# Regrouping the attention visits of a fused attention and maxout kernel, with one store per output tile

## The chip, the cores and the metric

The kernel runs on one core of a Trainium2 chip. The metric is the device time of one execution in microseconds (us). Profiles come from one execution each; their span is some 2 us shorter than the device time of the same execution. "State" below means whether an execution ran undisturbed (fast) or not (slow); with one core a profile shows that only through the time of the repeats, which agreed within about 1% unless said otherwise.

## The reference, cut to what matters

Eight batches, 12 heads, 448 positions, head width 64. A softmax attention with one extra term in the denominator is followed by a feed-forward layer that takes the maximum of three products ("experts").

```python
q, k, v: (8, 12, 448, 64) float32          # w1, w2, w3: (768, 768), w_out: (768, 768)

scores = (q @ k.T) / sqrt(64)
m = max(scores);  e = exp(scores - m)
attn = e / (sum(e) + exp(-m) + 1e-09)
x = (attn @ v) -> (3584, 768)              # batch and position by head and width
h = maximum(maximum(x @ w1, x @ w2), x @ w3)
out = h @ w_out                            # (3584, 768) float32
```

Of the kernel before, what the change touches and what calls it, by code (L numbers as in the profile page):

```python
# [16 lines left out]
MMDT = FP16  # L17
LAMBDA = 256.0


@with_exitstack
def kernel(
# [36 lines left out]
    LAST = 6  # L59
# [10 lines left out]
    ps_s = ctx.enter_context(tc.tile_pool(name="ps_s", bufs=3, space=bass.MemoryType.PSUM))  # L70
    ps_b = ctx.enter_context(tc.tile_pool(name="ps_b", bufs=2, space=bass.MemoryType.PSUM))

    ctx.enter_context(tc.manual_schedule())

# [97 lines left out]
    def warm(n, cols=512):  # L172
        ps = ps_b.tile([128, 512], FP32, tag="b", name="warm")
        for _ in range(n):
            nc.tensor.matmul(
                out=ps[:, 0:cols], lhsT=wz[:, 0:128], rhs=wz[:, 0:cols], start=True, stop=True
            )
# [14 lines left out]
    def transpose_pe(i, pr, pool, k_eng, q_engs):  # L192


        def tile_of():
            if pool is ps_s:
                return ps_s.tile([128, 2, 1024], MMDT, tag="s", name="trT")[:, 0]
            return ps_b.tile([128, 1024], MMDT, tag="b", name="trT")
# [23 lines left out]
    def transpose_once(i, nm, eng):  # L222

        if i not in KT:
            KT[i] = att_pool.tile([P, T * 128], MMDT, tag="KT", name="KT")
            QT[i] = att_pool.tile([P, (NB + 1) * 128], MMDT, tag="QT", name="QT")
        tp = ps_b.tile([128, 1024], MMDT, tag="b", name="trT")
        for b in range(T):
            nc.tensor.transpose(  # L229
                out=tp[:, ts(b, 128)],  # L230
                in_=raw[i][nm][:, 2 * b + 1 : 2 * b + 3, :].rearrange("x t d -> x (t d)"),
                identity=ident16,
            )
        dst = KT[i][:, 0 : T * 128] if nm == "k" else QT[i][:, 4 * 128 : (4 + T) * 128]
        evac(eng, dst, tp[:, 0 : T * 128])
# [54 lines left out]
    def scores(i, ej, units, part="EO"):  # L290
# [5 lines left out]
        for n in range(0, len(units), per):  # L296
            us = units[n : n + per]
            stp = ps_s.tile([128, 2, 512], FP32, tag="s", name="stp")
# [35 lines left out]
    def av_tail(i, ej, pr, ws=(0, 1, 2, 3)):  # L334

        eF, vt = e_buf[ej], vt_buf[i % NV]
        ps = ps_s.tile([128, 2, 512], FP32, tag="s", name="avp")
# [15 lines left out]
    def av_last(i, ej, pr):  # L353



        eF, vx, vt = e_buf[ej], v_buf[i % NV], vt_buf[i % NV]
        ps = avs[i, pr]

        def tile_mm(r, hh, o, rhs, stop):  # L360
            nc.tensor.matmul(  # L361
                out=ps[hh * HP : hh * HP + HP, r, 3 * D1 : 4 * D1],
                lhsT=eF[r * HP : r * HP + HP, o : o + HP],
                rhs=rhs,
                start=False,
                stop=stop,
                skip_group_check=True,
            )

        n = where[pr, None, TL]  # L370
        for hh in range(2):
            tile_mm(hh, hh, e_col(n, 3), vt[hh * HP : hh * HP + HP, pr, 0:D1], False)
        for c, x in enumerate((X1, X3, X2)):
            for r in range(2):
                for hh in range(2):
                    o = e_col(where[pr, hh, x], 3)
                    rhs = vx[r * HP : r * HP + HP, 2 * pr + hh, x[0], 0:D1]
                    tile_mm(r, hh, o, rhs, c == 2)

    def av_main(i, ej, pr, ws=(0, 1, 2, 3), last=False):  # L380
# [29 lines left out]
        if not last:  # L410
            return None
        end = small.tile([P, D1], FP32, tag="end", name="end")
        rl = small.tile([P, 1], FP32, tag="rl", name="rl")
        nc.scalar.activation(out=end, in_=ps[:, 1, 3 * D1 : 4 * D1], func=AF.Copy)  # L414

        def finish():
            nc.vector.tensor_tensor(out=end, in0=ps[:, 0, 3 * D1 : 4 * D1], in1=end, op=ALU.add)
            nc.vector.tensor_scalar(
                out=rl, in0=end[:, D:], scalar1=1.0 / LAMBDA, scalar2=None, op0=ALU.add
            )  # L420
            nc.vector.reciprocal(out=rl, in_=rl)  # L421
            for hh in range(2):
                h = slice(hh * HP, hh * HP + HP)
                nc.scalar.activation(  # L424
                    out=xn[i][0:HP, pr, 3, hh], in_=end[h, 0:D], func=AF.Copy, scale=rl[h]
                )

        return finish
# [14 lines left out]
    def x_transpose_pe(i, part):  # L443
# [3 lines left out]
        tp = ps_b.tile([128, NP, 2, 128], MMDT, tag="b", name="xtp")  # L447
# [10 lines left out]
    def x_transpose_all(i):  # L458
        b, g = groups[i]
        tp = ps_b.tile([128, NP, 4, 128], MMDT, tag="b", name="xtp")  # L460
# [20 lines left out]
    def up_piece(b, fcs, i, q0, qn):  # L481
# [5 lines left out]
        p_i = ps_b.tile([128, 512], FP32, tag="b", name="p_i")  # L487
# [18 lines left out]
    def out_piece(bp, t, c, w, queues):  # L506
# [5 lines left out]
        op_ps = ps_b.tile([128, 512], FP32, tag="b", name="op_ps")  # L512
# [12 lines left out]
        if queues is None:  # L525
            return
        for half in range(2):
            n = 2 * t + half
            b = 2 * bp + n // T
            rows = out[b * S : (b + 1) * S].rearrange("(p t) m -> t p m", t=T)[order[n % T]]  # L530
            queues[half].dma_start(
                out=rows[:, outs[1] : c + w], in_=o_sb[half * HP : half * HP + HP, outs[1] : c + w]
            )
        outs[1] = c + w
# [11 lines left out]
    def add_out(b):  # L546
        sy, sc = nc.sync, nc.scalar
        for t in range(0, 3) if b % 2 == 0 else range(3, 7):
            cuts = [(0, NW, None), (NW, NW, (sy, sy))]
            if b == B - 1 and t == 6:  # L550
                cuts = [(0, NW, (sy, sy)), (NW, 256, (sc, sc)), (NW + 256, 128, (sy, sc))]
            for c, w, queues in cuts:
                pieces.append((out_piece, (b // 2, t, c, w, queues), NFC * (w + 6)))
# [7 lines left out]
    def fill(cols):  # L561
        credit[0] += cols
        while pieces and credit[0] > 0:
            f, a, w = pieces.pop(0)
            f(*a)
            credit[0] -= w
        if not pieces:
            credit[0] = min(credit[0], 0.0)

    def one():  # L570
        if pieces:
            fill(max(0.0, 1.0 - credit[0]))
# [9 lines left out]
    def av(i, ej, pr, part):  # L582
        if i >= LAST:
            av_tail(i, ej, pr, (0, 1, 2))
            av_last(i, ej, pr)
            return av_main(i, ej, pr, (0, 1, 2), True)
# [24 lines left out]
    transpose_pe(0, 0, ps_s, DV, (AC, DV))  # L611
    attend("O", 0, S01)
    transpose_pe(0, 1, ps_b, DV, (DV,))
    attend("O", 0, S23, S46)
    warm(4)
    transpose_pe(1, 0, ps_b, AC, (DV,))
    transpose_pe(1, 1, ps_s, AC, (DV,))
# [5 lines left out]
    transpose_pe(2, 0, ps_b, AC, (DV,))  # L623
    transpose_pe(2, 1, ps_s, AC, (DV,))
# [34 lines left out]
    visits = ((0, 1), (2, 3), (4, 5, 6))  # L659
    adds = {3 * (3 * b + 4) + (b >= PE_X): b for b in range(1, B - 1)}  # L660
# [3 lines left out]
    def share(n):  # L664


        nxt = min([a for a in adds if a > n], default=3 * NI + 2)
        rest = range(n, nxt)
        sums = [AVC if m % 3 < 2 and m < 3 * NI else 0 for m in rest]
# [8 lines left out]
    for i in range(3, NI):  # L678
        ej, pj = (i + 1) % NEB, i % NEB
        first = i == 3  # L680
        if PE_QK <= i + 2 < NI:
            transpose_dma(i + 2)
        if first:
            load_v(i + 2)
        for vi, units in enumerate(visits):
            n = 3 * i + vi
            scores(i, ej, units)
            if i == 4 and vi == 0:
                prep_v(i, DV)
            finish = None  # L690
            if vi < 2:
                finish = av(i - 1, pj, vi, "E" if first else "EO")
            if n in adds:
                add_batch(adds[n])
            per = STEP if first and vi < 2 else share(n)
            if finish:
                one()
                finish()
            if vi == 1 and i > 3 * PE_X:
                x_transpose_dma(i - 1)  # L700
            if vi == 0 and first:
                x_transpose_pe(1, "E")
            if vi == 2 and first:
                x_transpose_pe(i - 1, "E")
                fill(per / 2)
                prep_v(i, DV)
                for w, cols in ((0, (0, NE)), (1, (0, NE)), (2, (NE, NO)), (2, (0, NE))):
                    add_up(0, *cols, [(w, f) for f in (0, 2, 4)])
                add_out(0)
                per = share(n)  # L710
            if vi == 2 and 3 < i <= 3 * PE_X:
                x_transpose_all(i - 1)
            if first:
                fill(per)
                per = 0
            if i + 1 < PE_QK and vi < 2:
                transpose_once(i + 1, "qk"[vi], (AC, DV)[vi])
            fill(per)
        if i + 1 < PE_QK:
            shift_q(i + 1, nc.gpsimd)  # L720
        if first:
            load_qk(i + 3)
        if i < 5:
            load_more(i + 3, i + 4)
        if 5 <= i + 1 < NI:
            prep_v(i + 1, nc.gpsimd)
        if PE_QK <= i + 2 < NI:
            shift_q(i + 2, nc.gpsimd)
        if i >= 5:
            load_more(i + 3, i + 4)  # L730

    for pr in range(NP):
        finish = av(NI - 1, NI % NEB, pr, "EO")
        one()
        finish()
    x_transpose_dma(NI - 1)
# [33 lines left out]
```

## The kernel before: the parts that the change and the argument touch

Everything is in 16-bit floats on TensorE, with float32 sums in PSUM. The heads are handled in groups of four (24 groups). The program is a hand-made schedule: **visits** of attention work (scores, exponentials, value products) alternate with **pieces** of feed-forward work from a list. There are two kinds of pieces: an expert piece is 6 matmuls of 448 columns, an output piece 6 matmuls of 384 columns. A third of a group's scores is worked on per visit, and the value products of a pair of heads in two of the three visits.

Two PSUM pools separate the two kinds of work; the sums of a visit never share a bank with a piece:

```python
ps_s = tc.tile_pool(name="ps_s", bufs=3, space=PSUM)     # scores and value sums, two banks each
ps_b = tc.tile_pool(name="ps_b", bufs=2, space=PSUM)     # pieces, one bank each
```

The value products of a pair. The last 64 queries (448 is 7 x 64, so one block of 64 is left over) come out as two half sums in two banks; ScalarE copies one, VectorE adds the other:

```python
def av_tail(...):   # small products: 64x64 tiles of TensorE
def av_last(...):   # the last 64 queries, in 64x64 tiles, two half sums
def av_main(i, ej, pr, ws, last=False):
    ...             # 18 wide products, 128x128
    # VectorE: rb = 1/(sum + 1/LAMBDA), then xn = acc * rb
    nc.scalar.activation(out=end, in_=ps[:, 1, 3 * D1 : 4 * D1], func=AF.Copy)
    def finish():
        nc.vector.tensor_tensor(out=end, in0=ps[:, 0, 3 * D1 : 4 * D1], in1=end, op=ALU.add)
        ...         # VectorE: rl = 1/(...); ScalarE: two scalings of 64x64
```

The output. One tile of `hT` holds 128 columns, that is two blocks of 64 positions; the positions of one block lie 7 rows apart in `out`. So each tile `o_sb` of 128 x 768 is stored as two transfers of 64 rows:

```python
def out_piece(bp, t, c, w, queues):
    ...             # 6 matmuls into a bank, VectorE scales into o_sb[:, c : c + w]
    for half in range(2):
        n = 2 * t + half
        b = 2 * bp + n // T
        rows = out[b * S : (b + 1) * S].rearrange("(p t) m -> t p m", t=T)[order[n % T]]
        queues[half].dma_start(out=rows[:, outs[1] : c + w],
                               in_=o_sb[half * HP : half * HP + HP, outs[1] : c + w])
```

SyncE (SP) issues these stores, and also the **DMA transposes**: transfers that turn a block of queries and keys (`QT<-ld_q`, `KT<-ld_k`) or of attention output (`xT<-xn`) on the way, so that TensorE need not do it.

The softmax here doesn't subtract the row's maximum and nothing guards it: scores larger than these inputs give would overflow.

## Time and profile before

| | before |
|---|---|
| device time, median of the first 3 runs (lowest to highest) | 339.3 us (338.11 to 339.39) |
| span of the profiled run | 336.9 us |
| mean granted TensorE clock | 0.999 |
| last matmul starts, end of the span | 331.38, 336.88 us |

The busy shares, the slices and the chain of waits of this kernel are in the prediction below. What the argument needs beside them are the clock row of the 40 slices (tenths of full speed in each), two rows of the list of DMA issues (KB of each, us from issue to landing), and TensorE's wait for a DMA transpose (us in total, how often, the longest):

```profile
PEclk9999999999999999999999999999999999999999
...
out_dram<-o_sb SPq DMA_DIRECT2D x54, 192.0 KB, 4.0
...
xT<-xn SPq DMA_TRANSPOSE x18, 4.8
```

```profile
PE p_i L490 <- DMA xT<-xn: 0.3, 1, 0.3
```

TensorE waits for a DMA transpose once, for 0.3 us.

```profile
L473 SPq DMA_TRANSPOSE xT<-xn x18: 1232/1233/2319, 85.3 to 300.1; - x18
```

### The profile page before, as it was taken

How to read it: one execution, taken by the hardware profiler on the slowest of the kernel's cores; microseconds unless marked ns; L12 is line 12 of the kernel's file. 1: busy time of each engine (PE TensorE's matmuls, PEld its weight loads, DVE VectorE, ACT ScalarE, POOL GpSimd, SP SyncE). 2: the span in 40 equal slices, each digit the busy share in tenths (PEclk: the TensorE clock that was granted, in tenths of full speed). 3: DMA queues.
4: the chain of work that ended last, by engine and by line, in shares of the span. 5: the costliest groups of instructions: out<-in, count | busy, mean ns of one | idle time of the engine just before them, and what ended most of it. 6: DMA issues, size and time to landing. Idle time of an engine off the chain costs nothing.

```text
span 336.9 us, 10248 instructions
## 1 busy us (share of the span) xinstructions
PE 326.1 (97%) x4316; PEld 195.9 (58%) x4316; DVE 199.9 (59%) x521; ACT 183.1 (54%) x289; POOL 146.7 (44%) x260
## 2 busy tenths in 40 slices
PE   7899999999999999999999999999999999999993
PEld 3668788866556655565546646555556555565552
DVE  4556675566566556556656556556556556575552
ACT  4768856655665755676556655666565665420000
POOL 8596578880671539170854328351754000000000
PEclk9999999999999999999999999999999999999999
DMA  8999999799799999969996999989990730124016
GB/s 141 197 200 207 203 205 191 128 161 191 109 108 132 171 234 145 124 96 190 177 156 81 114 259 120 150 99 220 186 149 18 164 89 2 31 47 129 0 33 157
DMA packets 84815, 46.46 MB, mean 138 GB/s; under 512 B 53280, under 2 KB 81312, under 8 KB 84768
## 3 DMA queue, kind: packets, MB, share of 16 engines
q0 software_dynamic: 29120, 21.80, 48.6%
q1 hardware_dynamic: 55264, 23.60, 41.3%
q8 instruction: 34, 0.56, 0.7%
q10 hardware_dynamic: 384, 0.39, 0.4%
q14 instruction: 13, 0.11, 0.1%
HBM read 44.04 MB, written 11.01 MB: 163 GB/s over the span
## 4 chain that ended last, share of the span: by engine, by line
PE 87%; DMA 5%; ACT 2%; DVE 2%; issue 1%; POOL 1%; POOLq 0%; ACTq 0%
PE p_i L490 48%; PE op_ps L514 14%; PE stp L304 11%; PE avp L388 9%; DMA xT<-xn 3%; ACT e L324 2%; DMA ld_q<-in_q_dram 2%; PE avp L344 2%; PE avp L361 1%; DVE xn L404 1%; PE trT L229 1%; DVE QT L190 1%; PE xtp L463 0%; ACT QT L188 0%; DVE rb L401 0%
## 5 line engine op out<-in xcount | busy, mean ns | idle before, releaser
L324 ACT ACTIVATE e<-stp 128x896 f16<-128x896 f32 (+4 forms) x171 | 143.9, 901 | 60.3 <-PE stp L304 60.1
L490 PE MATMUL p_i<-xT,w 128*128 128x448 f16 (+2 forms) x972 | 173.1, 332 | 0.5 <-DMA xT<-xn 0.3
L490 PEld LDWEIGHTS <-w 128*128 128x128 f16 x972 | 90.2, 98 | 69.1 <-issue 6.0
L249 POOL COPY QT<-QT 64x384 f16<-64x384 f16 (+1 forms) x84 | 46.9, 558 | 93.9 <-DMA QT<-ld_q 69.2
L501 DVE TENSOR_TENSOR hT<-hT,p_i 128x448 f16<-128x448 f16 (+2 forms) x96 | 59.7, 622 | 35.7 <-PE p_i L490 35.6
L514 PE MATMUL op_ps<-w,hT 128*128 128x384 f16 (+2 forms) x342 | 58.5, 323 | 0.0
L304 PE MATMUL stp<-QT,KT 64*64 64x448 f16 (+2 forms) x756 | 48.1, 338 | 2.6 <-ACT e L324 0.9
L499 DVE CAST hT<-p_i 128x448 f16<-128x448 f32 (+2 forms) x48 | 30.0, 625 | 25.2 <-PE p_i L490 25.2
L514 PEld LDWEIGHTS <-hT 128*128 128x128 f16 x342 | 32.0, 98 | 22.4 <-issue 2.0
L424 ACT ACTIVATE xn<-end,rl 64x64 f16<-64x64 f32 x72 | 24.9, 346 | 34.5 <-DVE rl L421 34.1
L521 DVE TENSOR_SCALAR o_sb<-op_ps 128x384 f32<-128x384 f32 (+2 forms) x57 | 31.2, 547 | 17.4 <-PE op_ps L514 16.8
L388 PE MATMUL avp<-vx,e 128*128 128x65 f16 x936 | 38.6, 194 | 0.0
L388 PEld LDWEIGHTS <-e 128*128 128x128 f16 x936 | 32.1, 97 | 2.3
L304 PEld LDWEIGHTS <-KT 64*64 64x64 f16 x756 | 15.8, 105 | 26.8 <-issue 23.9
L398 DVE TENSOR_SCALAR rb<-avp 128x6 f32<-128x6 f32 (+2 forms) x54 | 8.8, 164 | 36.8 <-PE avp L388 36.8
L404 DVE TENSOR_TENSOR xn<-avp,rb 128x384 f16<-128x384 f32 (+2 forms) x54 | 29.3, 543 | 1.8
L433 POOL COPY vx<-ld_v 128x768 f16<-128x768 f16 x21 | 17.2, 820 | 6.8 <-issue 4.2
L344 PEld LDWEIGHTS <-e 64*64 64x64 f16 x624 | 13.7, 107 | 8.1 <-issue 1.7
L102 POOL DMA_DIRECT2D ld_q<-in_q_dram x24 | 17.4, 723 | 2.3 <-DMA w<-in_moe_w_dram 1.1
L102 POOL DMA_DIRECT2D ld_k<-in_k_dram x24 | 17.3, 722 | 2.1 <-DMA w<-in_moe_w_out_dram 1.1
L414 ACT ACTIVATE end<-avp 128x65 f32<-128x65 f32 x36 | 8.2, 227 | 17.1 <-PE p_i L490 12.4
L115 POOL DMA_DIRECT2D ld_v<-in_v_dram x24 | 15.2, 634 | 2.6 <-DMA w<-in_moe_w_dram 1.3
(52 smaller groups left out, 162.1 us busy)
## 6 DMA issues: line engine op xcount, KB each, us to landing
out_dram<-o_sb SPq DMA_DIRECT2D x54, 192.0 KB, 4.0
ld_v<-in_v_dram POOLq DMA_DIRECT2D x48, 128.0 KB, 5.1
ld_k<-in_k_dram POOLq DMA_DIRECT2D x23, 224.0 KB, 6.6
ld_q<-in_q_dram POOLq DMA_DIRECT2D x23, 224.0 KB, 7.5
w<-in_moe_w_dram POOLq DMA_DIRECT2D x9, 384.0 KB, 9.2
w<-in_moe_w_out_dram POOLq DMA_DIRECT2D x3, 384.0 KB, 8.5
xT<-xn SPq DMA_TRANSPOSE x18, 4.8
QT<-ld_q SPq DMA_TRANSPOSE x17, 7.3
```

The source lines that it names most:

```text
L102: nc.gpsimd.dma_start(out=tiles[nm][:, 1 : NP * T + 1].rearrange("x (r t) d -> x r (t d)", r=NP)[:, p0:p1], in_=src[:, p0:p1],)
L249: eng.tensor_copy(out=t[d0 : d0 + HP, o * 128 : (o + n) * 128], in_=t[s0 : s0 + HP, a * 128 : (a + n) * 128],)
L304: nc.tensor.matmul(out=stp[half * HP : half * HP + HP, par, j * qn : (j + 1) * qn], lhsT=k_block(i, pr, h2, x[half]), rhs=q_cols(i, pr, h2 ...
L324: nc.scalar.activation(out=dst, in_=src, func=AF.Exp, scale=scale)
L388: nc.tensor.matmul(out=ps[:, hh, j * D1 : (j + 1) * D1], lhsT=eF[:, o : o + 128], rhs=vx[:, 2 * pr + hh, (x[0]), 0:D1], start=False, stop= ...
L404: nc.vector.tensor_tensor(out=xn[i][:, pr, ws[0] : ws[0] + nw].rearrange("p j h d -> p h j d"), in0=acc[:, :, :, 0:D], in1=rb.unsqueeze(3) ...
L424: nc.scalar.activation(out=xn[i][0:HP, pr, 3, hh], in_=end[h, 0:D], func=AF.Copy, scale=rl[h])
L490: nc.tensor.matmul(out=p_i[:, j * qn : (j + 1) * qn], lhsT=w_sb[i][:, dc, ts(fc, 128)], rhs=xT[b][:, dc, q0 : q0 + qn], start=(dc == 0), s ...
L499: nc.vector.tensor_copy(out=dst, in_=src)
L501: nc.vector.tensor_tensor(out=dst, in0=dst, in1=src, op=ALU.max)
L514: nc.tensor.matmul(out=op_ps[:, 0:w], lhsT=hT[bp][:, fc, ts(t, 128)], rhs=wout_sb[:, fc, c : c + w], start=(fc == 0), stop=(fc == NFC - 1),)
L521: nc.vector.tensor_scalar(out=o_sb[:, c : c + w], in0=op_ps[:, 0:w], scalar1=1.0 / LAMBDA, scalar2=None, op0=ALU.mult,)
```

## The change

Its intent has four parts: fewer, fuller visits from group 6 on (three groups, 21 score units, in seven visits of three units, where there were nine); all sums of a pair of heads in one PSUM bank, one of the two that pieces use, in turn; the last 64 queries of a pair scaled by VectorE straight from that bank, one piece later; and each output tile stored by one transfer. The core of the diff:

```diff
-    ps_s = ctx.enter_context(tc.tile_pool(name="ps_s", bufs=3, space=bass.MemoryType.PSUM))
-    ps_b = ctx.enter_context(tc.tile_pool(name="ps_b", bufs=2, space=bass.MemoryType.PSUM))
+    slots = [ps.tile([128, 2, 512], FP32, name=f"ps{j}") for j in range(3)]
+    banks = [ps.tile([128, 512], FP32, name=f"pb{j}") for j in range(2)]
...
+    def visit(units, pair):
...
+            for at in anti:                       # scores of the first unit on two of the four tiles
+                s0(*at)
+            turned = turn_over(smalls(diag, True))   # first half of the small products on the others
+            for s, at in ((s0, diag), (s1, anti), (s1, diag), (s2, anti), (s2, diag)):
+                for corner in at:
+                    s(*corner)
+            smalls(anti, False, turned)           # second half, behind a semaphore
...
+            wides()
...
         def finish():
+            for hh in range(2):
+                nc.vector.tensor_scalar(out=dst[0:HP, pr, 3, hh], in0=acc[h, 6, 0:D],
+                    scalar1=rb[h, 6:7], scalar2=None, op0=ALU.mult)
+            if pr == 1:
+                x_transpose_dma(pi)
+        if units:
+            return finish                         # called after the next piece
+        finish()
...
-        for half in range(2):
-            n = 2 * t + half
-            b = 2 * bp + n // T
-            rows = out[b * S : (b + 1) * S].rearrange("(p t) m -> t p m", t=T)[order[n % T]]
-            queues[half].dma_start(
-                out=rows[:, outs[1] : c + w], in_=o_sb[half * HP : half * HP + HP, outs[1] : c + w]
-            )
+        r0, r1 = ((2 * bp + n // T) * S + order[n % T] for n in (2 * t, 2 * t + 1))
+        cols = slice(outs[1], c + w)
+        for p0, r, k in ((0, r0, 2),) if r1 > r0 else ((0, r0, 1), (HP, r1, 1)):
+            at = out[r : r + 1, cols]
+            rows = bass.AP(
+                at.tensor, at.offset, [[abs(r1 - r0) * DM, k], [T * DM, HP], [1, c + w - outs[1]]]
+            )
+            queue.dma_start(out=rows, in_=o_sb[p0 : p0 + k * HP, cols])
```

The pattern in `out` has three dimensions, slowest first: `k` = 2 blocks, 64 rows, the columns. The bytes are those of the two transfers before. In one tile of seven the second block lies ahead of the first (`r1 < r0`), and that tile keeps two transfers.

## The prediction

That matmuls overlap is meant as the trace of before shows it: one of an expert product takes 352 ns there and the next starts 0.189 us after it. And a transpose on TensorE, put at 0.066 us in step 4, starts 0.056 us after the one ahead of it at the median of that trace.

> **What bounds the kernel now.** I read the page from the top: busy shares, the 40 slices, then the chain of work that ended last.
>
> ```profile
> PE 326.1 (97%) x4316; PEld 195.9 (58%) x4316; DVE 199.9 (59%) x521; ACT 183.1 (54%) x289; POOL 146.7 (44%) x260
> PE   7899999999999999999999999999999999999993
> DMA  8999999799799999969996999989990730124016
> PE 87%; DMA 5%; ACT 2%; DVE 2%; issue 1%; POOL 1%; POOLq 0%; ACTq 0%
> ```
>
> TensorE is 97% busy, full in all but the first two slices and the last, and carries 87% of the chain. Busy alone is weak evidence, since matmuls overlap, so I compared starts of consecutive matmuls in the trace: after the first 13 us no two lie more than 0.6 us apart, save once, at 194.3 us, where an expert product waited for a transpose (0.65 us instead of 0.19; the list of waits books 0.3 us). So the end is set by how densely TensorE's stream is packed. DVE, ACT and POOL have 40% and more to spare; a saving there is worth something only if TensorE waits for it. The DMA engines are full to about 280 us, but only that one wait shows.
>
> How dense is one visit? The timeline of TensorE over one of them (start, us, engine, line, operation), with the vector engine's part behind it:
>
> ```profile
> 201.61 0.35 PE L490 MATMUL p_i<-xT,w 128*128 128x448 f16 x1
> 201.90 0.57 PE L304 MATMUL stp<-QT,KT 64*64 64x448 f16 x8
> 202.30 0.26 PE L344 MATMUL avp<-vt,e 64*64 64x65 f16 x12
> 202.42 0.27 PE L361 MATMUL avp<-vx,e 64*64 64x65 f16 x10
> 202.62 0.74 PE L388 MATMUL avp<-vx,e 128*128 128x65 f16 x18
> 203.20 3.57 PE L490 MATMUL p_i<-xT,w 128*128 128x448 f16 x18
> ...
> 203.40 0.16 DVE L398 TENSOR_SCALAR rb<-avp 128x6 f32<-128x6 f32 x1 [0.78 <-PE avp L388]
> 203.60 0.19 DVE L401 RECIPROCAL rb<-rb 128x6 f32<-128x6 f32 x1
> 203.82 0.56 DVE L404 TENSOR_TENSOR xn<-avp,rb 128x384 f16<-128x384 f32 x1
> 204.53 0.62 DVE L499 CAST hT<-p_i 128x448 f16<-128x448 f32 x1 [0.15 <-PE p_i L490]
> ```
>
> A visit is a stretch in 64x64 tiles (scores, small value products), then 128x128 work: 18 wide value products, then expert pieces of 6 matmuls. Expert matmuls start every 0.189 us (18 in 3.40 us in the chain). The first score starts 0.29 us after the last expert matmul (201.61 to 201.90): **0.09 us to enter tile mode**. Starts in the trace give 0.124 us from the last small product to the first wide one where the cadence is 0.03: **0.09 us to leave it**; from a score straight to an expert piece it is 0.27 instead of 0.19, so 0.08. A set of four scores takes 0.19 us, 26 small products 0.23.
>
> [...]in this visit a small product starts at 202.395 on one tile, ahead of the one that precedes it in the program[...].[...]
>
> **The change, part by part.** I listed TensorE's instructions in both programs: 4316 matmuls each.
>
> 1. *Fewer visits.* Stretches in tile mode fall from 82 to 70: some 13 score-only ones go (an exit of 0.08 and an entry of 0.09 each), and the last pair of heads now needs two stretches instead of one. 12 x 0.18 = **2.2 us less**.
>
> 2. *Packing inside a stretch.* Each now holds three score units and both halves of the small products. The small ones on the diagonal tiles run beside the first unit's anti-diagonal scores. A diagonal tile has three scores (3 x 0.187) and 7 small products (7 x 0.031), 0.78 us; before, three units and a pair's small ones took 3 x 0.19 + 0.23 = 0.80. Over 37 such visits some **0.3 us less**, counting the entry effects.
>
> 3. *Semaphore between the two halves.* The second half (other row tiles, same bank) waits for a scalar-engine instruction that waits for the first half. From the stretch's start: first half done at 0.19 + 0.19 latency, then three steps of about 0.05 each (early scores start 0.05 after what releases them): 0.53 us. The second half is due at about 0.57. An estimate of **0.5 us more** for all visits.
>
> 4. *Group 5* takes the new form: 12 wide products fewer (0.03 each) and 8 PE transposes fewer (0.066 each): **0.9 us less**. Its transpose becomes a DMA, needed about 8 us after issue; landings of that kind take 4.4 to 8.6 us at that time.
>
> 5. *Scaling of the last 64 queries.* ACT loses 36 copies (8.2 us) and 72 scalings (24.9 us); DVE loses 36 x (218 + 154 + 164) ns = 19.3 us and gains 76 scalings of 64x64. Off TensorE's path, so nothing by itself. But the sums' bank is now one of the two that pieces use, and is free only after these scalings, which stand behind the first piece's copy. That is a **new wait**, and the program has it: the last piece of a visit waits for the second scaling. With U the first piece's start: its copy starts at U+1.33 (203.20 to 204.53) and takes 0.62. A scaling costs 0.225 us, an estimate from the PSUM forms of one op (292 ns at 128 columns, 425 at 256: 1.04 ns a column). So the bank is free at U+2.40, and TensorE restarts at U+2.45.
>  - In a visit of three 448-column pieces the third is due at U+2.27: 0.18 us lost. Program order shows 17 such: **3.1 us more**.
>  - Visits of four pieces or more lose nothing (due at U+3.09 or later).
>  - The first three new visits have only 1, 2 and 2 output pieces of 0.97 us. There the scalings end at about U+2.2 (the copy waits for the 0.56 us product that ends at U+1.18), while the next user of the bank is due at U+0.97 or 1.07: 1.2 + 1.3 + 1.3 = **3.7 us more**.
>
> 6. *The wait at 194 us* should go: a batch's pieces now begin 9.5 to 11 us after its last transpose is issued, 7.5 to 9.5 before. **0.4 us less**.
>
> 7. *Stores.* Six output tiles of seven go out in one transfer instead of two (the seventh's rows run backwards and keep two); bytes are equal. Hidden, except at the end:
>
> ```profile
> 330.10 3.88 SPq L531 DMA_DIRECT2D out_dram<-o_sb  x5
> 330.49 1.43 DVE L521 TENSOR_SCALAR o_sb<-op_ps 128x384 f32<-128x384 f32 x3 [0.42 <-DMA out_dram<-o_sb]
> ...
> 331.60 1.84 ACTq L531 DMA_DIRECT2D out_dram<-o_sb  x3
> ```
>
>  The last data are ready at 331.92, but the queue is still issuing and starts the last store at 333.51; it lands 2.1 us later. The tile ahead of the last still needs two transfers, the last one fewer: the last store should start some 0.6 to 1.0 us earlier. **0.6 us less**.
>
> Sum: -2.2 - 0.3 + 0.5 - 0.9 + 3.1 + 3.7 - 0.4 - 0.6 = +2.9 us, 342.2.
>
> **Rivals.**
> - *The waits are hidden, only the switches count.* For it: TensorE waits for almost nothing now, and the change was evidently laid out to keep it so. Against it: the waits are in the program, and their times follow from durations in the trace. It would give 339.3 - 4.4 + 0.5, about 335.5.
> - *Tile packing fails*: small products do not run beside longer scores on other tiles, or the semaphore takes longer. Up to 0.19 us in 37 visits, 7 us: about 346 to 349. The out-of-order start above speaks against it; no trace of before has unequal lengths side by side in different tiles for long.
> - *A transfer becomes the bound.* The DMA engines are 90% busy for most of the run. Shifted copies of the queries stay 12 us and more ahead of their use in the late groups (from the trace), so I give this little; group 5's transpose might cost 1 us.
> - *ACT or DVE relief brings time.* ACT is 54% busy and no TensorE wait of note ends on it: nothing.
>
> **Range and chances.** The mechanism sum is 342.2. The first rival pulls down by 6 us and I give it a quarter; packing failure pulls up by as much with about a tenth. I predict 341.0 us, with 336.5 to 345.0 for 8 in 10. Faster by over 2% needs 332.5, less than switches alone explain: 0.03. Slower by over 2% needs 346.1, the packing failure: 0.07. Within 2%: 0.90.
>
> **What would show it.** In the changed profile: 70 tile stretches with entry and exit still near 0.09; the scores' first part and the small products starting within 0.01 us of each other, and about 0.87 us from first score to first wide product; gaps of about 0.2 us before the third piece in 17 visits, listed as waits of the expert product on the vector engine, and three gaps of over 1 us near 80 to 90 us; scalings of about 0.22 us; no wait near 195 us; the last store issued within 1 us of the last copy. I am wrong if the expert products show no wait on the vector engine (then 335 to 337), or if the stretch takes over 1 us (then 346 and more).

## More of the kernel before

How long SP was held by each store and each transpose is in the two views by source line (minimum, median and maximum in ns, then the first and last start in us):

```profile
L531 SPq DMA_DIRECT2D out_dram<-o_sb x57: 466/587/1661, 70.0 to 333.5; - x57
```

## The result, and the profile after

| | before | after |
|---|---|---|
| device time, median (lowest to highest) | 339.16 us (338.11 to 339.39, 4 runs) | 428.28 us (426.27 to 431.2, 4 runs) |
| ratio after to before | | 1.264 (95% interval 1.256 to 1.272) |
| span of the profiled run | 336.9 us | 426.0 us |
| mean granted clock | 0.999 | 0.915 |
| last matmul starts, end of the span | 331.38, 336.88 us | 402.83, 426.01 us |

A ratio here is the mean time of one kernel's fast runs over that of the other's of the same rounds, so it is not quite the ratio of the medians that are quoted. Executions over 1.5% slower than the fastest of the same kernel are left out of the means. The change made the kernel 26% slower; the prediction had 0.5% and gave "slower by over 2%" a chance of 0.07.

The page of the changed kernel, the rows that answer to those shown before (busy shares, slices of TensorE, clock and DMA, the list of DMA issues):

```profile
PE 345.0 (81%) x4316; PEld 206.3 (48%) x4316; DVE 202.5 (48%) x488; ACT 149.8 (35%) x181; POOL 146.4 (34%) x260
...
PE   8899998609999989799496995949799997499800
...
PEclk9999999957999999999796996969989998879965
DMA  9999999999995959859898499993997292710121
...
out_dram<-o_sb SPq DMA_DIRECT2D x23, 384.0 KB
```

The same 4316 matmuls, but the row of TensorE now has holes, and behind most holes the clock row has a dip: 5, 7, 6. Two slices at the end are empty. TensorE's list of waits says what it stood for:

```profile
PE pb L595 <- DMA xT<-xn: 29.9, 5, 11.6
PE pb L482 <- issue: 6.2, 2, 4.0
PE ps L415 <- POOL QT L268: 5.4, 1, 5.4
PE ps L415 <- DMA KT<-ld_k: 5.0, 1, 5.0
PE pb L619 <- DVE xn L524: 2.3, 2, 1.1
```

Transposes that land late head it: of attention output (`xT`), of queries (`QT`, through POOL's copies) and of keys (`KT`). Only the last row, 2.3 us, is a wait that the prediction spoke of. In the row "issue" TensorE waited for nothing that the profile shows. The lists of waits of this run and of e2 to e4 have 14 such waits, of up to 4.6 us; those of the runs without slow stores have none. What TensorE waited for there is not shown. The timeline around the first hole (start, us, engine, line, operation; SPq is SP's time to issue) shows how it comes about:

```profile
78.98 0.52 SPq L639 DMA_DIRECT2D out_dram<-o_sb  x1
...
79.69 10.30 SPq L260 DMA_TRANSPOSE QT<-ld_q  x1
...
90.08 3.07 SPq L260 DMA_TRANSPOSE KT<-ld_k  x1
...
94.98 0.91 PE L595 MATMUL pb<-xT,w 128*128 128x448 f16 x2 [11.61 <-DMA xT<-xn]
...
95.67 2.82 PE L595 MATMUL ps<-xT,w 128*128 128x448 f16 x7
```

A store goes out, and the transpose issued next holds SP for 10.30 us. An expert product then waits 11.6 us for its own transpose. That one had been issued before this store: SP began it at 75.04 us and was done with it at 78.87, and it landed only 16 us later. Once TensorE runs again, seven matmuls take 2.82 us, 0.38 each where they start every 0.19 us at full clock. Over the whole run, by source line (stores, then transposes of attention output and of queries):

```profile
L639 SPq DMA_DIRECT2D out_dram<-o_sb x33: 511/561/9486, 70.8 to 407.1; - x33
```

```profile
L578 SPq DMA_TRANSPOSE xT<-xn x19: 1260/2687/13586, 75.0 to 363.8; - x19
```

```profile
L260 SPq DMA_TRANSPOSE QT<-ld_q x17: 1220/1227/17900, 55.3 to 322.0; - x17
```

Set against the same views of the kernel before: the stores' longest issue went from 1.7 to 9.5 us, that of the transposes of attention output from 2.3 to 13.6. Those of queries took at most 4.1 us before and up to 17.9 now.

**Where the 89 us of span went.** Nine holes in TensorE's stream, 2.4 to 12 us each, sum to about 49 us. Behind eight of them the clock stays at about 0.5 while matmuls run, for 33 us in all; half of that, some 16 us, is lost. (These 33 us are the stretches of low clock less the part in which TensorE still waited.) From the last matmul to the end it is 23.2 us instead of 5.5: 17.7 us. The other parts of the change cost 6.0 us, as the first experiment shows. 49 + 16 + 17.7 + 6 is 89.

Behind seven of the nine holes, those of 4 us and more, the granted clock in this trace is 0.5, and full again 2.7 to 5.9 us after TensorE resumes. The hole of 3.1 us at 174.3 us has no dip, that of 2.4 us at 351.3 us has one (0.50 from 353.7 to 356.9 us), so the length of the hole alone does not settle it. Its place goes with it here: the clock's steps in this trace lie whole multiples of 3.413 us apart (at 87.23, 206.69 and 353.47 us, for example). Counted in windows of that length from one step, each of the eight drops came at the end of a window in which a hole took about 2.0 us or more; the short hole put 2.0 us into one window. The hole of 3.1 us was split over two windows, 1.3 and 1.4 us, and no drop followed. In all, a late transfer is paid for one and a third times here ((49 + 16) / 49).

**Why the store.** The trace's packet records hold the stores as packets of 3072 bytes (one row), 128 for a tile. Counting how many are in flight, for groups of stores that lie apart from others:

| kernel | slowest dimension in `out` | packets at once, mean | time for the 128 packets of a tile |
|---|---|---|---|
| before | 64 | 8.4 to 15.5 | 1.0 to 2.8 us |
| after | 2 | 1.8 to 2.0 | 8.0 to 9.3 us |

One packet takes the same in both, 0.12 us at the median. What changed is how many are on their way at once. The transposes' packets, of 256 bytes, are at times over 20 at once in both kernels (28 at most), so they were not held to two. No record names the engine that moves a packet, so how a store of two packets at a time makes the transposes beside it late is not shown. Whether it does is for the experiments.

### The profile page after: what moved, and what is told of

The parts are those of the page before. It is cut to its first block, busy times and chain, and to the rows that moved or that the text cites. A ratio compares the mean times of both kernels' runs of the same rounds, so it can differ in the third digit from the quotient of the medians.

```text
span 426.0 us, 10223 instructions
## 1 busy us (share of the span) xinstructions
PE 345.0 (81%) x4316; PEld 206.3 (48%) x4316; DVE 202.5 (48%) x488; ACT 149.8 (35%) x181; POOL 146.4 (34%) x260
## 5 line engine op out<-in xcount | busy, mean ns | idle before, releaser
L426 ACT ACTIVATE e<-ps 128x896 f16<-128x896 f32 x126 | 106.5, 917 | 179.9 <-PE ps L415 163.0
L595 PE MATMUL pb<-xT,w 128*128 128x448 f16 (+2 forms) x696 | 133.6, 337 | 31.8 <-DMA xT<-xn 29.9
L595 PE MATMUL ps<-xT,w 128*128 128x448 f16 x276 | 62.5, 374 | 0.0
L415 PE MATMUL ps<-QT,KT 64*64 64x448 f16 x504 | 43.4, 364 | 11.9 <-POOL QT L268 5.4
L604 DVE CAST hT<-pb 128x448 f16<-128x448 f32 (+2 forms) x40 | 25.0, 625 | 51.3 <-PE pb L595 50.3
L606 DVE TENSOR_TENSOR hT<-hT,pb 128x448 f16<-128x448 f16 (+2 forms) x58 | 36.0, 621 | 25.9 <-PE pb L595 23.1
L343 ACT ACTIVATE e<-ps 128x896 f16<-128x896 f32 (+4 forms) x45 | 36.4, 869 | 18.3 <-PE ps L323 18.0
L619 PE MATMUL pb<-w,hT 128*128 128x384 f16 (+2 forms) x198 | 35.7, 321 | 2.5 <-DVE xn L524 2.3
L482 PE MATMUL pb<-vx,e 128*128 128x65 f16 x684 | 29.3, 196 | 6.2 <-issue 6.2
L619 PE MATMUL ps<-w,hT 128*128 128x384 f16 x144 | 25.5, 326 | 0.0
```

The source lines that it names most:

```text
L343: nc.scalar.activation(out=dst, in_=src, func=AF.Exp, scale=scale)
L415: return nc.tensor.matmul(out=stp[half * HP : half * HP + HP, par, 0:S], lhsT=k_block(i, pr, h2, x[half]), rhs=q_cols(i, pr, h2, par, "EO" ...
L426: nc.scalar.activation(out=dst, in_=stp[:, :, 0:S], func=AF.Exp, scale=scale)
L482: nc.tensor.matmul(out=ps[:, (3 * hh + j) * D1 : (3 * hh + j + 1) * D1], lhsT=eF[:, o : o + 128], rhs=vx[:, 2 * pr + hh, (x[0]), 0:D1], st ...
L595: nc.tensor.matmul(out=p_i[:, j * qn : (j + 1) * qn], lhsT=w_sb[i][:, dc, ts(fc, 128)], rhs=xT[b][:, dc, q0 : q0 + qn], start=(dc == 0), s ...
L604: nc.vector.tensor_copy(out=dst, in_=src)
```

## The experiments

**Theories.** S: the store's pattern, 2 in the slowest dimension and about two packets at a time for 384 KB, delays the transposes beside it and the end of the run; everything else in the change is as predicted. Q: the stores hold SP's queue, and the transposes are late because SP issues them late; another queue mends it. V: the new visits (bank turns, fuller stretches) open the holes, or make the stores harmful. L: one large transfer as such is the trouble, not its pattern. e2, e3 and e4 are single executions, whose state is unknown; they are 76 to 111 us above the kernel before, where the repeats of one kernel lie within 6 us.

### e1: the changed kernel, two transfers per tile again

```diff
-        for p0, r, k in ((0, r0, 2),) if r1 > r0 else ((0, r0, 1), (HP, r1, 1)):
+        for p0, r, k in ((0, r0, 1), (HP, r1, 1)):
```

> The changed kernel with one part undone: each output tile goes out by two transfers of 64 rows again, same queue. Theory A[...]: time falls from 428 to 341 to 344 us, the value that the prediction's other terms give without its tail gain; no TensorE wait of over 1 us on a transpose is left; the granted clock is back at 0.99 or more; the waits on the scalings of 64 queries stay (three of about 1.3 us near 70 to 80 us, some 17 of 0.23 us). Rival B (the transposes are late because the change issues them at other places between the visits): stays above 400 us.

Theory A, here and in e2, is S above.

Measured: 344.73 us (344.64 to 345.43, 4 runs), before 339.42; ratio 1.017 (1.012 to 1.021). Span 342.9, clock 0.999. The busy shares and slices of e1:

```profile
PE 327.1 (95%) x4316; PEld 200.3 (58%) x4316; DVE 202.6 (59%) x488; ACT 149.8 (44%) x181; POOL 146.4 (43%) x260
...
PE   7899899978999999999999999999999999999993
...
PEclk9999999999999999999999999999999999999999
```

The holes, the low clock and the long end are gone with one line: 83 of the 89 us are the store. What is left, a 7 in slice 9 (69 to 77 us), is two of the three waits of over 1 us that the prediction expected. The time is 0.7 us above the range of this expectation.

### e2: the kernel before with the merged store alone

```diff
-        for half in range(2):
-            ...                                   # two transfers of 64 rows
+        for p0, r, k in ((0, r0, 2),) if r1 > r0 else ((0, r0, 1), (HP, r1, 1)):
+            ...                                   # as in the change
+            queues[0].dma_start(out=rows, in_=o_sb[p0 : p0 + k * HP, cols])
```

> The kernel before with that one part alone: output tiles stored by one transfer where the rows allow it, visits as before. Theory A: slower by much, 400 us or more, with packets of 3072 bytes about 2 at a time and TensorE waiting for transposes. Rival B: stays within 2% of 339 us, since the visits and the places of the transposes are those of before.

Measured (one look): 415.61 us, before 339.42. Span 413.8, clock 0.91. TensorE's waits in e2:

```profile
PE stp L304 <- DMA KT<-ld_k: 30.9, 3, 12.5
PE p_i L490 <- DMA xT<-xn: 12.5, 1, 12.5
```

So it does not take the new visits: the old kernel slows by 76 us with this store alone. The waits fall on other transposes (keys more than attention output), and the longest, 12.5 us, is like the 11.6 us above. V is out as a cause.

### e3: the merged stores issued from ScalarE's queue

```diff
-            queue.dma_start(out=rows, in_=o_sb[p0 : p0 + k * HP, cols])
+            nc.scalar.dma_start(out=rows, in_=o_sb[p0 : p0 + k * HP, cols])
```

> The changed kernel, single transfers kept, but issued from the scalar engine's queue in place of the sync engine's, so that the transposes no longer stand behind them in one queue. If order within one queue does the harm: most of the loss goes, 345 to 370 us, although the stores still go 2 packets at a time.[...] The scalar engine's exponentials may be held up by its own store issues: then the loss shows there.

Measured (one look): 439.42 us; span 437.6, clock 0.909. TensorE's waits in e3, and the transposes by source line:

```profile
PE pb L453 <- ACTq L473: 24.8, 8, 6.1
PE pb L595 <- DMA xT<-xn: 17.5, 2, 8.8
```

```profile
L578 SPq DMA_TRANSPOSE xT<-xn x19: 1232/1234/5584, 75.4 to 370.8; - x19
```

SP now issues these transposes at the old median, 1.23 us, and TensorE still waits 17.5 us for their landing. So another queue does not mend it, as Q would have it: transposes issued as fast as before, most of them, still land late. The longest of these issues on SP fell from 13.6 to 5.6 us, and a new wait came on ScalarE, which now issues the stores and where the program has a semaphore instruction that TensorE's small products wait for (24.8 us). So a part of Q may stay true, that whoever issues these stores is held by them; how long each issue held ScalarE was not read. e3 is 11 us slower than the changed kernel.

### e4: plain two-dimensional stores, 62 + 2 rows

Each half tile goes out in two transfers with two-dimensional patterns: 62 rows and 2 rows.

```diff
-        for p0, r, k in ((0, r0, 2),) if r1 > r0 else ((0, r0, 1), (HP, r1, 1)):
-            ...
+        for p0, r in ((0, r0), (HP, r1)):
+            for j, n in ((0, 62), (62, 2)):
+                at = out[r + j * T : r + j * T + 1, cols]
+                rows = bass.AP(at.tensor, at.offset, [[T * DM, n], [1, c + w - outs[1]]])
+                queue.dma_start(out=rows, in_=o_sb[p0 + j : p0 + j + n, cols])
```

> The changed kernel with plain two-dimensional stores, but each half tile split into 62 rows and 2 rows.[...] 410 to 450 us like the changed kernel, 3072-byte packets about 2 at a time. If it is the three-dimensional pattern of the single transfer: 341 to 350 us like two transfers of 64 rows, plus some issue time for twice the transfers.

The first range is what S gives. That 62 rows would go out like 2 was the assumption.

Measured (one look): 450.44 us; span 448.7, clock 0.899. Packets at once 1.7 to 2.0; the first tile took 10.0 us. TensorE's waits in e4:

```profile
PE pb L595 <- DMA xT<-xn: 33.8, 5, 12.2
PE ps L415 <- DMA KT<-ld_k: 19.4, 3, 10.4
```

No third dimension and no transfer of over 186 KB, and it is as bad: a slowest dimension of 62 or 2 goes out about two packets at a time here, where one of 64 had 8.4 to 15.5 in the kernel before. So neither the third dimension nor the size is needed for the harm. What sets 62 apart from 64 is not shown.

### e5: one transfer per tile, to 128 consecutive rows

The opposite: one transfer of 384 KB whose slowest dimension is 128. It puts the rows in the wrong order within their batch. The comparison with the reference cannot tell these row orders apart, and says nothing about their order in any run here.

```diff
-        for p0, r, k in ((0, r0, 2),) if r1 > r0 else ((0, r0, 1), (HP, r1, 1)):
-            ...
+        at = out[(7 * bp + t) * 128 : (7 * bp + t) * 128 + 128, outs[1] : c + w]
+        queue.dma_start(out=at, in_=o_sb[:, outs[1] : c + w])
```

> The changed kernel with every output tile stored by one transfer, but to 128 consecutive rows, so that the slowest dimension is 128 on both sides; the rows land in the wrong places on purpose, so the result is wrong. If the harm is in the outer dimension of 2, one transfer as such is harmless: 343 to 345 us, within 0.5% of two transfers (344.7), less the tail gain that was predicted for fewer transfers (0.6 us), packets of 3072 bytes 10 or more at a time. If one transfer of 384 KB as such holds the transposes up: 400 or more.

Measured: 343.55 us (343.36 to 343.78), before 338.85; ratio 1.013 (1.011 to 1.016). Span 341.7. Its list of DMA issues, and the stores by source line:

```profile
out_dram<-o_sb SPq DMA_DIRECT2D x27, 384.0 KB, 5.0
```

```profile
L633 SPq DMA_DIRECT2D out_dram<-o_sb x29: 332/332/2744, 70.8 to 338.5; - x29
```

Packets at once 4.8 to 14.3, a tile in 1.1 to 3.7 us. L falls: one transfer of 384 KB is harmless, with 332 ns for most issues. Its median and its span are each 1.2 us below e1's (spans 341.7 and 342.9). The two ran on different chips, and the intervals of their ratios overlap, so this gain is not shown. The intent of the store was sound, its pattern was not. A correct store with 64 slowest and 2 next, the order that these runs speak for, needs the rows of the two blocks to alternate in `o_sb`. The direct try (reading `hT` in that order as the stationary operand) does not build: the build refused that operand with its two free dimensions. So no run shows a correct store of this kind.

### i1: e1 with the last 64 queries scaled at once

The remaining 5 us should be the two waits of step 5 of the prediction: pieces that need the sums' bank before the deferred scalings have freed it.

```diff
-        if units:
-            return finish
         finish()
```

> Two transfers as in the first experiment, and the last 64 queries scaled at once, ahead of the first piece's copy. The trace with two transfers shows 17 third pieces 0.23 us late on the scalings (3.9 us) and three waits of 1.02, 1.30 and 1.30 us in the first new visits. Theory: the 17 go, and the three shrink to about 0.8 us each: 344.7 - 3.9 - 1.3 = 339.5 us. Rival: the copy of the first piece now comes 0.6 us later and holds up something else: no gain or less than half.

Measured: 340.97 us (340.03 to 345.16, the highest over 1.5% above the lowest), before 338.85; ratio 1.005 (1.002 to 1.008). Span 338.9. So the deferral costs 4.0 us of span, less than the 5.2 expected.

### i2: i1 with more pieces for short visits

A visit's share of the pieces is the mean over what is left, less an allowance for its own sums. A negative allowance gives the first three new visits more pieces than their 1, 2 and 2; none gives the last visit five.

```diff
-        sums = [AVC if plan[m][1] else 0 for m in rest]
+        sums = [(-2400 if NV0 <= m < NV0 + 3 else 0 if m == len(plan) - 1
+                 else AVC if plan[m][1] else 0) for m in rest]
```

> As the one before, and the pieces shared out so that the first three new visits get more of them (two double ones, two, four in place of one, two, two) and the very last one gets five in place of four. Theory: of the three waits one of about 0.8 us is left, 1.6 us less; the wait of 0.8 us for the last transpose ahead of the last batch goes: 339.5 - 2.4 = 337.1 us. Rival: the double pieces go through two banks only, and earlier visits with fewer pieces become too short for the scalar engine: as much lost there.

Measured: 338.17 us (338.01 to 338.22), ratio 0.997 (0.994 to 1.000). Span 336.5: another 2.4 us, as expected; the time itself is 1.1 us above the 337.1 given.

### i3: i2 with the last stores on two queues

```diff
-            cuts = [(0, NW, None), (NW, NW, sy)]
+            cuts = [(0, NW, None), (NW, NW, (sy, sc) if b == B - 1 and t == 5 else (sy, sy))]
...
-                cuts = [(0, NW, sy), (NW, 256, sc), (NW + 256, 128, sy)]
+                cuts = [(0, NW, (sy, sc)), (NW, 256, (sy, sc)), (NW + 256, 128, (sy, sc))]
```

> As the one before, and the last two tiles' stores split over the sync and the scalar engine's queues. In the kernel before, the last data were ready 1.6 us before the last store was issued. Theory: 0.8 us less, 336.3 us, which is under the kernel before (339.4) by 0.9%. Rival: the landing, not the issue, ends the run: no change.

Measured: 338.15 us (338.02 to 340.1, 6 runs), before 338.85 (12 runs, one slow at 343.73); ratio 0.998 (0.996 to 1.001). A miss: the last store is issued at 332.60 us and lands at 334.81, and the time is that of i2. i3's longer waits of TensorE on pieces:

```profile
PE pb L617 <- DVE xn L524: 0.6, 1, 0.6
PE ps L617 <- DVE hT L604: 0.6, 2, 0.3
...
PE pb L593 <- DVE KT L211: 0.4, 1, 0.4
```

The second row is a wait that e1 did not have: with the scalings at once, VectorE's copy of the last expert piece comes later, and the output piece that reads it stands twice for 0.44 us (by the starts of the matmuls).

### i4: scalings at once in short visits only

```diff
+            if finish and len(ahead) <= 3:        # three pieces or fewer: scale at once
+                finish()
+                finish = None
         fill(per, finish if units else None)      # otherwise one piece later
```

and -1500 in place of -2400, which gives the first new visits 2, 3 and 3 pieces.

> The kernel of i3_tail_on_two_queues with two edits: the scaling of the last 64 queries is done at once only where the visit has three pieces or fewer, behind the first piece otherwise; and the first three new visits get 2, 3 and 3 pieces. Theory (what is left in the time beside the store's pattern is single waits of TensorE, and each counts in full): the two waits of 0.44 us at 182.7 and 258.4 us (an output piece that waits for a copy held up by the scalings) and part of the 0.76 us at 71.0 us go, nothing comes in their place, so about 0.9 to 1.3 us less than the 338.15 of i3: 336.9 to 337.3, ratio to before 0.994 to 0.996. Rival (with nothing on TensorE's path waiting for it, the new order only moves the waits to the sums' bank): the same as i3 within 0.3 us, with new waits of 0.2 us or so ahead of third pieces.

Measured: 336.32 us (335.89 to 336.83, 6 runs), before 338.5 (337.98 to 340.77, 11 runs); ratio 0.992 (0.989 to 0.995). All its waits of TensorE on pieces:

```profile
PE pb L595 <- DVE xn L524: 0.3, 1, 0.3
```

All three rows of i3 are gone (the row here stood in i3 too, at 67 us). By the starts of the matmuls, gaps of 0.53, 0.76, 0.44 and 0.44 us have closed, 2.2 us, and the span fell by 1.8 (336.2 to 334.4), somewhat more than expected. This version beats both kernels: before by 0.8%, which is small, but the interval is clear of 1.

## Why the prediction was wrong, point by point

**The step that failed is step 7**, "Stores ... bytes are equal. Hidden, except at the end", and with it the rival "A transfer becomes the bound", of which it said "I give this little". It counted bytes and issues, and took the time on the engines as given by the bytes. The runs show the term it left out: a tile's 128 packets went from 1.0 to 2.8 us, 8.4 to 15.5 at once, to 8.0 to 9.3 us, about two at once. This was not hidden, because the transposes that TensorE needs land late beside such stores (TensorE waited up to 11.6 us for one); by what path is not shown. e2 shows that the store alone does it, e1 that without it 83 us go away, e4 and e5 that it goes with the slowest dimension (2 or 62 against 128) and not with the size of a transfer. The "0.6 us less" at the end became 17.7 us more.

That the DMA engines were busy for most of the run was read, in the prediction, as a sign that they cope. The slack it quoted for shifted queries, 12 us and more, is of the same size as the delays that came (five transposes of queries held SP for 10.3 to 17.9 us), so it was no safety.

The other steps can be checked in e1, which is the change without its store. They summed to +3.5 us without step 7's gain (342.8); e1 has 344.73.

1. *Fewer visits*, right: 70 stretches in tile mode instead of 82.
2. *Packing* and 3. *semaphore*, right in size: 0.92 us from the first score to the first wide product against the 0.87 expected (median of 37). From the lengths of the stretches in both traces, points 1 to 3 together save an estimated 2 us (1.6 to 2.4, by how the waits inside them are set apart), where the prediction's terms sum to 2.0. The second half of the small products starts 0.60 us after the stretch begins, expected 0.57. "Tile packing fails" did not come about: the timeline of e1 has scores and small products starting together.

```profile
178.58 0.38 PE L415 MATMUL ps<-QT,KT 64*64 64x448 f16 x2
178.58 0.31 PE L453 MATMUL pb<-vt,e 64*64 64x65 f16 x8
...
179.49 0.73 PE L482 MATMUL pb<-vx,e 128*128 128x65 f16 x18
```

4. *Group 5*: TensorE's only late transpose in e1 is that of point 6, so none was lost here; the 0.9 us of this term was not measured by itself.
5. *Scaling of the last 64 queries*, right in mechanism, a little small: the third piece is 0.23 us late in 17 visits (3.9 us; expected 0.18, 3.1 us); a scaling takes 279 ns and not the estimated 225. The list of waits, where the prediction meant to see them, has none of the 17: TensorE was idle for only 0.07 us before each, and that list starts at 0.15. The first three new visits wait 1.02, 1.30 and 1.30 us (expected 1.2, 1.3, 1.3). These are 7.5 us, with the late transpose of the next point 8.3; i1 and i2 act on them and took 6.4 us of span away, less than that, since waits came in their place (the rows of i3).
6. *The wait at 194 us* went in e1, as said. But the last batch's transpose is 0.81 us late in e1 (it landed at 308.88 us, the product started at 308.91), where the prediction had nothing; it had named a late transpose only for group 5, at 1 us at most. It is gone in i2, whose five pieces give it time.

Points 5 and 6 were 0.7 and 0.8 us above their terms, which is most of the 1.9 us between 342.8 and 344.7; how the rest splits is open.

So without the store, the first rival ("the waits are hidden") is wrong too, and the range of 336.5 to 345.0 would have held e1, with 0.3 us to spare. The mechanism sum was close; the term that decides was not in it.

## What to carry to other kernels

Before merging two transfers, write down the slowest dimension of both patterns, and count in a trace how many packets are on their way at once. Here stores with 64 or 128 slowest had 4.8 to 15.5 at once, those with 2, or with 62 and 2, about two; with 2, equal bytes took three to nine times as long as with 64 (8.0 to 9.3 us against 1.0 to 2.8). Other sizes were not run. Here the slow transfer cost less by its own end (17.7 us) than through the transposes beside it (49 us of holes and 16 us of clock); so ask of a store, which nobody waits for, whose transfers run beside it. Deferring work "off the path" is free only if nobody needs the buffer that it holds: i4 gained by deciding that per visit.
